# A fused window attention and SwiGLU kernel on one core: group 1 loaded and transposed earlier, sink tables on GpSimd

## The chip, the core and the metric

The kernel runs on one core of a Trainium2 chip. A core has five engines that work side by side, each through its own instruction list in order: TensorE (PE in the profile, its weight loads PEld), VectorE (DVE), ScalarE (ACT), GpSimd (POOL) and SyncE (SP). GpSimd issues most of the loads here, because they turn float32 in memory into bfloat16 on the chip; SyncE issues stores, transposing transfers and a few small loads. Products of TensorE land in PSUM, of which the kernel uses eight banks.

The metric is the device time of one execution, in microseconds (us). The time before is the median of nine executions.

## The reference

Attention of 4 batches, 8 heads, 768 tokens and head size 64, with a window of 128 tokens and 4 sink tokens that every later token sees, and behind it a gated feed-forward block:

```python
scores = scale * np.matmul(q, k.transpose(0, 1, 3, 2))
keep = (pos[None, :] < n_sink) | ((rel >= 0) & (rel < window))
a = softmax(np.where(keep, scores, -1e9))
x = np.matmul(a, v).transpose(0, 2, 1, 3).reshape(B * S, H * D)   # 3072 x 512
g = x @ w_gate                                                    # 512 x 1536
out = (g * sigmoid(g) * (x @ w_val)) @ w_out                      # 1536 x 512
```

Inputs and output are float32; the kernel multiplies in bfloat16.

## The kernel before

**Groups.** The tokens form 12 groups of 256, three for each batch; group g is batch g // 3. Attention goes by groups, in steps whose names the lists below use:

- `step_T(g, ph)`: transposes of keys and queries by TensorE (L257), half of the heads for each `ph`; the key half is copied out of PSUM by ScalarE, the query half by VectorE (L263). Groups 0 to 3 only. Later groups are transposed by transfers on SyncE's queue (`cross_T`, L285; in the lists it is `C(g)`).
- `step_S(g, p2)`: scores of four heads (L323), their exponentials on ScalarE (four of them, L330), and the multiplication with the window mask on VectorE (two of them, L335).
- `step_K(g)`: scores against the four sink tokens of the batch (L346) and their exponential `es` (L350). Not for the first group of a batch, whose window mask holds the sinks. `step_ks(b)` makes the sink keys, and, on VectorE (L300), `vsb`: the sink values laid out so that one product adds them for four heads. It multiplies `vcf`, which eight small loads on SyncE's queue fill (L190), with the pattern `diag_h`.
- `step_PV(g, j, hh)`: probabilities times values for one half of the heads and one tile of 128 tokens; where sinks apply, the product with `es` and `vsb` comes first in the accumulation. The result is divided by the row sum, on VectorE (L375, L382), or on ScalarE where `act` is set (L378).
- `step_X(g, j)`: transposes the 128 x 512 result into `xT` (L406), copied out by VectorE (L412) or, with `act`, by ScalarE (L410).

**Chunks.** The feed-forward block takes the tokens in eight chunks of 256 or 512 (`SIZES`). `gate(tb, f)` makes the gate and the value projection of chunk `tb` (L434), a tanh on ScalarE (L441) and two products on VectorE (`u` L447, `ht` L448). `down(tb, ts)` multiplies with `w_out` (L480), and ScalarE copies out (L484).

**Order.** Everything is emitted in an order written out by hand; each engine keeps to it. A preamble does group 0. Then `weave(us, slots(...))` walks over a list `us` of gates and downs; each number in `slots` is a place in that list, and the attention steps named there are emitted inside that gate (between its two projections) or spread over that down. `alone` is a place with attention only. Copies out of PSUM and mask multiplications are put into a list `later`, which `flush` empties, so that they come behind the current gate's own work. `us` here is g0[0], `alone`, three more gates of chunk 0, the six of chunk 1, the last two of chunk 0, and then downs and chunk 2. `warm(n)` issues matmuls on zeros, whose results nobody reads.

**Loads.** GpSimd issues them in the order of the program: k of group 0, v of group 0, the first piece of the two gate weights (`wg0`, `wv0`), k and q of group 1, the second piece, v of group 1, the other weight pieces. q of group 0 comes over the queues of ScalarE and SyncE. Behind the preamble come group 2, `w_out`, groups 3 and 4; `next_load(g)` loads group g + 4. Bank allocation: all PSUM tiles share one rotation of eight.

Of the kernel before, what the change touches and what calls it, by code (L numbers as in the profile page):

```python
# [15 lines left out]
def kernel(  # L16
# [75 lines left out]
    def load4(g):  # L92

        x = natp.tile([P, H, 4 * D], BF16, tag="kq", name="kq")
        for i, src in ((0, k), (1, q)):
            nc.gpsimd.dma_start(
                x[64 * i:64 * (i + 1)], four_tokens(src, g, slice(0, H)))
        nat[g] = x
# [19 lines left out]
    def load_v(g):  # L118
        va = new_v(g)
        b, c = divmod(g, GC)  # L120
        for j in range(2):
            t0 = c * 256 + j * P
            nc.gpsimd.dma_start(  # L123
                va[:, j, :, 0:D], v[b, :, t0:t0 + P].rearrange("h m d -> m h d"))
# [3 lines left out]
    def load_gate(i):  # L128
        f0, n = sum(FCH[:i]) * P, FCH[i] * P
        for lst, w, nm in ((wgs, moe_w_gate, "wg"), (wvs, moe_w_val, "wv")):  # L130
            t = wpool.tile([P, DMC, n], BF16, tag=f"{nm}{i}", name=nm)
            nc.gpsimd.dma_start(
                t, w[:, f0:f0 + n].rearrange("(c p) f -> p c f", p=P))
            lst.append(t)
# [3 lines left out]
    def load_out(i):  # L138
        n = DFC // 4
        t = wpool.tile([P, n, DM], BF16, tag=f"wo{i}", name="wo")  # L140
        nc.gpsimd.dma_start(
            t, moe_w_out[i * n * P:(i + 1) * n * P].rearrange("(c p) f -> p c f", p=P))
        wos.append(t)
# [25 lines left out]
    for p in range(NP2):  # L169
# [11 lines left out]
    nc.gpsimd.iota(tk, [[0, 1]], base=0, channel_multiplier=1,  # L181
                   allow_small_or_imprecise_dtypes=True)
    load_v(0)
    load_gate(0)

    nc.vector.memset(vcf, 0.0)
    nc.vector.memset(vcf[:, :, D:D + 1], 1.0)
# [5 lines left out]
    for ks in kss:  # L193
# [7 lines left out]
    nc.gpsimd.affine_select(  # L201
        out=dh, in_=dh, compare_op=ALU.is_ge, fill=0.0, base=NS - 1,
        pattern=[[32, NP2], [NS, 2]], channel_multiplier=-1)
    load4(1)
    load_gate(1)
    load_v(1)
    for i in range(2, 5):
        load_gate(i)

    def build_masks():  # L210
# [12 lines left out]
    kTs, qTs, es_t, e_t, xns, xTs = {}, {}, {}, {}, {}, {}  # L223
    later = []

    def flush():
        for f in later:
            f()
        later.clear()

    def warm(n):

        ps = bank([P, 512], FP32, "wm")
        for _ in range(n):
            nc.tensor.matmul(ps, wm[:, 0:P], wm, start=True, stop=True)

    def step_T(g, ph):

        if ph == 0:
            new_kq(g)  # L240
        own = lambda i, p: nat[g][:, 2 * p:2 * p + 2]
        transpose(g, ph, own, (ident, ident))

    def new_kq(g):
        kTs[g] = kqtp.tile([P, NP2, 256], BF16, tag="kT", name="kT")
        qTs[g] = kqtp.tile([P, NP2, 256], BF16, tag="qT", name="qT")

    def transpose(g, ph, rows, ids):


        pts = [bank([P, 2, 64, 4], FP32, "pt") for _ in range(2)]
        for p in range(2):
            for r in range(4):
                for h in range(2):
                    for i in range(2):
                        o = slice(64 * i, 64 * (i + 1))
                        nc.tensor.matmul(  # L257
                            pts[i][64 * h:64 * (h + 1), p, :, r],
                            rows(i, 2 * ph + p)[o, h, r * D:(r + 1) * D],
                            ids[i][o, o], start=True, stop=True)  # L260
        for i, (dst, copy) in enumerate(((kTs, nc.scalar.copy),
                                         (qTs, nc.vector.tensor_copy))):
            copy(out=dst[g][:, 2 * ph:2 * ph + 2],  # L263
                 in_=pts[i].rearrange("q a m r -> q a (m r)"))

    def keys(b, t, r, p):

# [22 lines left out]
    def step_ks(b):  # L290

        dst = kss[b].rearrange("q (a m) -> q a m", m=KS)
        for h in range(2):
            r = slice(h * D, (h + 1) * D)
            nc.vector.tensor_copy(
                out=dst[r, :, h * NS:(h + 1) * NS],
                in_=kTs[b * GC][r, :, 0:NS] if b * GC < NPE
                else cross[b * GC][r, 0, 0, :, 0:NS])
        vsb = const.tile([P, H, D + 1], BF16, tag=f"vsb{b}", name="vsb")
        nc.vector.tensor_tensor(  # L300
            vsb,
            vcf[:, b:b + 1].broadcast_to([P, H, D + 1]),
            diag_h.rearrange("q (h o) -> q h o", o=1).broadcast_to([P, H, D + 1]),
            op=ALU.mult)
        vsbs.append(vsb)

    def step_S(g, p2):

        b, c = divmod(g, GC)
# [42 lines left out]
    def step_PV(g, j, hh, act=False):  # L352
        b, c = divmod(g, GC)
        t = 2 * c + j
        if hh == 0:
            xns[g, j] = xnp.tile([P, DM], BF16, tag="xn", name="xn")
        po = bank([P, 4, D + 1], FP32, "o")
        mms = []
        if c > 0:
            mms.append((po, es_t[g][:, j * P:(j + 1) * P],  # L360
                        vsbs[b][:, 4 * hh:4 * hh + 4]))
        for hq in range(4):
            h = 4 * hh + hq
            if t > 0:
                vp = vas[g][:, 0, h, 0:D + 1] if j else vas[g - 1][:, 1, h, 0:D + 1]
                mms.append((po[:, hq], e_t[g][:, h, 256 * j:256 * j + P], vp))
            mms.append((po[:, hq], e_t[g][:, h, 256 * j + P:256 * (j + 1)],
                        vas[g][:, j, h, 0:D + 1]))
        for i, (o, l, r) in enumerate(mms):
            nc.tensor.matmul(o, l, r, start=(i == 0), stop=(i == len(mms) - 1),  # L370
                             skip_group_check=True)

        def dve():
            rcp = smallp.tile([P, 4, 1], FP32, tag="rcp", name="rcp")
            nc.vector.reciprocal(rcp, po[:, :, D:D + 1])  # L375
            if act:
                for h in range(4):
                    nc.scalar.activation(  # L378
                        xns[g, j][:, (4 * hh + h) * D:(4 * hh + h + 1) * D],
                        po[:, h, 0:D], AF.Copy, scale=rcp[:, h])  # L380
                return
            nc.vector.tensor_tensor(  # L382
                xns[g, j][:, 256 * hh:256 * (hh + 1)].rearrange(
                    "p (h d) -> p h d", h=4),
                po[:, :, 0:D], rcp.broadcast_to([P, 4, D]), op=ALU.mult)
        later.append(dve)
        if hh == 1 and g >= NXPE:
            later.append(lambda: nc.sync.dma_start(
                x_tile(g, j), xns[g, j], transpose=True))
# [106 lines left out]
    def downs(tb):  # L496
        return [(down, tb, t) for t in range(SIZES[tb] // P)]

    def A(fn, *a):
        return lambda: fn(*a)  # L500

    def next_load(g):
        if g + 4 < NG:
            (load4 if g + 4 < NPE else load1)(g + 4)
# [2 lines left out]
    def sinks(b):  # L507
        return [lambda: later.append(A(step_ks, b))]

    def T(g):  # L510
        def last():
            step_T(g, 1)
            next_load(g)
        return [A(step_T, g, 0), last]

    def Ss(g):
        return [A(step_S, g, p2) for p2 in range(2)]

    def PVs(g):

        return [A(step_PV, g, j, hh) for hh in range(2) for j in range(2)]

    def Xs(g):
        return [A(step_X, g, j) for j in range(2)]

    def K(g):
        return A(step_K, g)
# [6 lines left out]
    def pro(*steps):  # L534
        for s in steps:
            s()
            if len(later) > 1:
                later.pop(0)()
# [9 lines left out]
    def C(g):  # L548

        def last():  # L550
            cross_T(g)
            next_load(g)
        return [last]
# [11 lines left out]
    step_S(0, 0)  # L565
    warm(1)
    step_S(0, 1)
    warm(3)
    pro(*[lambda: None] * 3)
    step_PV(0, 0, 0)  # L570
    step_PV(0, 1, 0)
    flush()
    step_PV(0, 1, 1, True)
    step_PV(0, 0, 1)
    flush()
    warm(2)
    pro(A(step_X, 0, 0), A(step_X, 0, 1, True))
    flush()
    warm(2)
    step_ks(0)  # L580
    load4(2)
    load_v(2)
    for i in range(4):
        load_out(i)
    for g in (3, 4):
        (load4 if g < NPE else load1)(g)
        load_v(g)


    g0, g1, g2 = gates(0), gates(1), gates(2)  # L590
    us = [g0[0], (alone, 0, 0), *g0[1:4], *g1, *g0[4:6], downs(0)[0], *g2,
          downs(0)[1], *downs(1), *downs(2)]
    p1 = [A(step_PV, 1, j, hh, j == 1) for hh in range(2) for j in range(2)]
    weave(us, slots(
        (0, T(1)), (1, Ss(1) + [K(1)]), (3, p1 + [flush]),
        (4, [A(step_X, 1, 0), A(step_X, 1, 1, True), flush]),
        (8, T(2)), ((9, 10), Ss(2)), (10, [K(2)]),
        (11, PVs(2)[:2] + [flush]), (12, PVs(2)[2:] + [flush]), (12, C(4)),
        (13, [A(step_X, 2, 0), A(step_X, 2, 1, True), flush]),
        (14, T(3)), ((15, 16), Ss(3)), (16, sinks(1)), ((17, 17, 18, 18), PVs(3)),  # L600
        (18, C(5)), (19, Xs(3)), ((20, 21), Ss(4)), (21, [K(4)]),
        ((22, 22, 23, 23), PVs(4)), (24, Xs(4))))


    def pair(ga, gb, sh=0):
        s = sh
# [46 lines left out]
```

## Time and profile before

| What | Value |
|---|---|
| Median of nine runs | 248.35 us (247.96 to 249.72) |
| Profiled execution | 249.72 us, its span 248.0 us |
| PE busy | 235.1 us, 95% of the span |
| DVE busy | 162.0 us, 65% |
| ACT busy | 112.4 us, 45% |
| POOL busy | 66.6 us, 27% |
| Granted clock of TensorE, mean | 0.991 |
| Loads on GpSimd's queue | 13.90 MB, last one issued near 119 us |

The profile shows one execution. Its span begins with the first instruction and is 1.7 us shorter than the time that the device reports. A row of a timeline gives start, length, engine, line of the kernel, what is written and read, and in brackets how long the engine had stood still and what ended that. Slices cut the span into 40 equal parts of 6.2 us; a digit is the busy share in tenths.

### The profile page before, as it was taken

What the parts mean: (1) busy time and instruction counts of PE and PEld (TensorE: products, weight loads), DVE (VectorE), ACT (ScalarE), POOL (GpSimd) and SP (SyncE); (2) the same over time, 40 slices, a digit from 0 to 9 for tenths busy, and PEclk for the clock granted to TensorE, in tenths of its full rate; (3) what the DMA queues carried; (4) which work ended last, traced back from release to release, by engine and by line L of the source; (5) the groups of instructions that cost most, each with busy time, mean ns of one, the idle gap of its engine ahead of it and who ended that gap; (6) DMA issues with size and microseconds to landing.
All of it is one profiled execution on the core that took longest, in us unless ns stands there. A gap on an engine that the chain in (4) does not pass through costs nothing.

```text
span 248.0 us, 5200 instructions
## 1 busy us (share of the span) xinstructions
PE 235.1 (95%) x2073; PEld 135.8 (55%) x2086; DVE 162.0 (65%) x341; ACT 112.4 (45%) x225; POOL 66.6 (27%) x88
## 2 busy tenths in 40 slices
PE   7689999999699999999999999999999999999994
PEld 3457786778435544544445454445454445488443
DVE  2777888859734288893298991199981289887100
ACT  2658548166063256541564721555611662333111
POOL 8956264893499208005200000000000000000000
PEclk9999999999889999999999999999999999999999
DMA  7999999999999999547990143900244200200132
GB/s 137 151 184 198 203 191 203 159 147 162 152 155 193 184 189 95 36 83 104 221 146 1 41 89 90 210 0 1 45 85 127 87 0 3 42 0 3 42 127 86
DMA packets 97704, 27.11 MB, mean 109 GB/s; under 512 B 83728, under 2 KB 94736, under 8 KB 97680
## 3 DMA queue, kind: packets, MB, share of 16 engines
q0 software_dynamic: 68832, 13.90, 68.4%
q1 hardware_dynamic: 28416, 12.49, 24.0%
q10 hardware_dynamic: 432, 0.39, 0.5%
q8 instruction: 16, 0.26, 0.5%
q14 instruction: 8, 0.07, 0.1%
HBM read 28.34 MB, written 6.29 MB: 140 GB/s over the span
## 4 chain that ended last, share of the span: by engine, by line
PE 77%; DVE 11%; ACT 6%; issue 2%; DMA 2%; POOL 0%; DVEq 0%; POOLq 0%
PE pd L480 24%; PE pv L434 22%; PE pg L434 20%; PE o L370 5%; ACT e L330 4%; DVE ht L448 3%; PE s L323 3%; DVE e L335 2%; DMA kq<-in_k_dram 2%; DVE u L447 2%; DVE xn L382 2%; PE pt L257 2%; PE pd L461 1%; PE px L406 1%; ACT xn L378 1%
## 5 line engine op out<-in xcount | busy, mean ns | idle before, releaser
L434 PE MATMUL pv<-xT,wv 128*128 128x256 bf16 (+1 forms) x384 | 74.8, 328 | 0.9 <-DVE ht L448 0.7
L434 PE MATMUL pg<-xT,wg 128*128 128x256 bf16 (+1 forms) x384 | 74.2, 326 | 0.2 <-ACT xT L410 0.2
L441 ACT ACTIVATE th<-pg 128x512 f32<-128x512 f32 x72 | 43.5, 607 | 61.4 <-PE pg L434 60.8
L447 DVE SCALAR_TENSOR_TENSOR u<-th,pg 128x512 bf16<-128x512 f32 x72 | 49.1, 682 | 30.0 <-ACT th L441 29.6
L480 PE MATMUL pd<-wo,ht 128*128 128x512 bf16 x264 | 63.6, 384 | 0.8 <-issue 0.2
L448 DVE TENSOR_TENSOR ht<-u,pv 128x512 bf16<-128x512 bf16 x72 | 49.5, 687 | 10.4 <-PE pv L434 3.8
L434 PEld LDWEIGHTS <-wg 128*128 128x128 bf16 x384 | 37.5, 98 | 26.0 <-issue 0.6
L330 ACT ACTIVATE e<-s 128x512 bf16<-128x512 f32 (+1 forms) x96 | 45.9, 580 | 7.5 <-PE s L323 7.4
L434 PEld LDWEIGHTS <-wv 128*128 128x128 bf16 x384 | 34.6, 98 | 20.9 <-issue 2.7
L480 PEld LDWEIGHTS <-ht 128*128 128x128 bf16 x276 | 26.2, 99 | 29.1 <-issue 1.4
L484 ACT ACTIVATE ot<-pd 128x512 f32<-128x512 f32 x23 | 13.8, 599 | 49.2 <-PE pd L480 49.1
L335 DVE TENSOR_TENSOR e<-e,mask 128x1024 bf16<-128x1024 bf16 (+1 forms) x48 | 29.3, 641 | 6.6 <-ACT e L330 6.4
L107 POOL DMA_DIRECT2D kq<-in_k_dram x16 | 14.2, 890 | 31.6 <-DMA kqT<-kq 26.9
L123 POOL DMA_DIRECT2D va<-in_v_dram x24 | 21.3, 896 | 4.5 <-DMA kq<-in_q_dram 2.5
L370 PEld LDWEIGHTS <-e 128*128 128x128 bf16 x352 | 16.3, 98 | 7.0 <-DVE e L335 2.0
L382 DVE TENSOR_TENSOR xn<-o,rcp 128x256 bf16<-128x256 f32 x45 | 19.1, 424 | 1.5
L370 PE MATMUL o<-va,e 128*128 128x65 bf16 x352 | 17.9, 193 | 1.3 <-DVE e L335 1.3
L107 POOL DMA_DIRECT2D kq<-in_q_dram x16 | 14.2, 890 | 5.7 <-DMA wo<-in_moe_w_out_dram 2.3
L375 DVE RECIPROCAL rcp<-o 128x4 f32<-128x4 f32 x48 | 8.2, 174 | 8.4 <-PE o L370 8.4
L263 DVE CAST qT<-pt 128x512 bf16<-128x512 f32 x8 | 5.2, 687 | 8.2 <-PE pt L257 8.1
L465 DVE TENSOR_SCALAR ot<-pd 128x256 f32<-128x256 f32 x1 | 0.4, 425 | 14.4 <-PE pd L461 14.4
L370 PE MATMUL o<-vsb,es 128*128 128x260 bf16 x32 | 8.8, 275 | 0.7 <-ACT es L350 0.7
(60 smaller groups left out, 107.9 us busy)
## 6 DMA issues: line engine op xcount, KB each, us to landing
out_dram<-ot SPq DMA_DIRECT2D x23, 256.0 KB
va<-in_v_dram POOLq DMA_DIRECT2D x24, 128.0 KB, 8.7
kq<-in_k_dram POOLq DMA_DIRECT2D x18, 128.0 KB, 7.3
kq<-in_q_dram POOLq DMA_DIRECT2D x16, 128.0 KB, 8.0
wo<-in_moe_w_out_dram POOLq DMA_DIRECT2D x4, 384.0 KB, 12.5
wg<-in_moe_w_gate_dram POOLq DMA_DIRECT2D x4, 256.0 KB, 8.8
wv<-in_moe_w_val_dram POOLq DMA_DIRECT2D x4, 256.0 KB, 9.1
kq<-in_k_dram POOLq DMA_DIRECT2D x3, 256.0 KB, 11.5
```

Of the source, the lines that this page charges most:

```text
L107: nc.gpsimd.dma_start(x[:, j, i].rearrange("p (h d) -> p h d", d=D), src[b, :, t0:t0 + P].rearrange("h m d -> m h d"))
L123: nc.gpsimd.dma_start(va[:, j, :, 0:D], v[b, :, t0:t0 + P].rearrange("h m d -> m h d"))
L330: nc.scalar.activation(e_t[g][:, h0 + h, lo:512], pss[2 * pp + h][:, lo:512], AF.Exp, scale=scale)
L335: nc.vector.tensor_tensor(e, e, m[:, :, lo:512].broadcast_to([P, 2, 512 - lo]), op=ALU.mult)
L370: nc.tensor.matmul(o, l, r, start=(i == 0), stop=(i == len(mms) - 1), skip_group_check=True)
L382: nc.vector.tensor_tensor(xns[g, j][:, 256 * hh:256 * (hh + 1)].rearrange("p (h d) -> p h d", h=4), po[:, :, 0:D], rcp.broadcast_to([P, 4, ...
L434: nc.tensor.matmul(ps[:, i * n:(i + 1) * n], ws[fi][:, c, fo * P:(fo + 1) * P], x[:, 0:n // P, c], start=(c == 0), stop=(c == DMC - 1))
L441: nc.scalar.activation(th, pg, AF.Tanh, scale=0.5)
L447: nc.vector.scalar_tensor_tensor(u, th, 1.0, pg, op0=ALU.add, op1=ALU.mult)
L448: nc.vector.tensor_tensor(hts[tb][:, f:f + two].rearrange("p a n -> p (a n)"), u, pv, op=ALU.mult)
L480: nc.tensor.matmul(po, hts[tb][:, f, ts * P:(ts + 1) * P], wos[f // n][:, f % n], start=(f == 0), stop=(f == DFC - 1))
L484: nc.scalar.activation(ot, po, AF.Copy, scale=0.5)
```

## The change

Loads: k and q of group 1 are issued ahead of the first weights, and v of group 1 ahead of the second. The sink tables `vsb` are built by GpSimd instead of VectorE: the table of batch 0 in the preamble, between v of group 1 and the second weights, the other three behind the loads of `w_out`. Group 1 is transposed in the preamble: its first half behind the context products of group 0, with both copies out of PSUM on ScalarE (`q_act`), its second half behind `step_X` of group 0, with the query copy put into `later` (`q_late`). The first half of the scores of group 1 is emitted in the preamble too. Three calls of `warm` (seven matmuls) become one (two), and two copies out of PSUM that ScalarE had in group 0 go to VectorE.

In the list of gates and downs, three gates of chunk 1 now stand ahead of the fourth of chunk 0, and both downs of chunk 0 ahead of chunk 2. The other attention steps have new places: the context products of group 1 in `alone` and the gate behind it, `step_X` of group 3 in a down instead of in the last gate of chunk 2, the first scores of group 4 in that last gate.

```diff
     load_v(0)
+    load4(1)
     load_gate(0)
+    def build_vsb(b):
+        vsb = const.tile([P, H, D + 1], BF16, tag=f"vsb{b}", name="vsb")
+        nc.gpsimd.tensor_tensor(
+            vsb,
+            vcf[:, b:b + 1].broadcast_to([P, H, D + 1]),
+            diag_h.rearrange("q (h o) -> q h o", o=1).broadcast_to([P, H, D + 1]),
+            op=ALU.mult)
+        vsbs.append(vsb)
...
-    load4(1)
-    load_gate(1)
     load_v(1)
-    for i in range(2, 5):
+    build_vsb(0)
+    for i in range(1, 5):
         load_gate(i)
...
+        evict(0, kTs, nc.scalar.copy)
+        q_copy = A(evict, 1, qTs, nc.scalar.copy if q_act else nc.vector.tensor_copy)
+        if q_late:
+            later.append(q_copy)
+        else:
+            q_copy()
...
     step_S(0, 1)
-    warm(3)
+    warm(2)
     pro(*[lambda: None] * 3)
     step_PV(0, 0, 0)
     step_PV(0, 1, 0)
     flush()
-    step_PV(0, 1, 1, True)
     step_PV(0, 0, 1)
+    step_PV(0, 1, 1)
+    step_T(1, 0, q_act=True)
     flush()
-    warm(2)
-    pro(A(step_X, 0, 0), A(step_X, 0, 1, True))
+    step_X(0, 0)
+    step_X(0, 1)
+    step_T(1, 1, q_late=True)
     flush()
-    warm(2)
     step_ks(0)
+    step_S(1, 0)
     load4(2)
     load_v(2)
     for i in range(4):
         load_out(i)
+    for b in range(1, B):
+        build_vsb(b)
...
-    us = [g0[0], (alone, 0, 0), *g0[1:4], *g1, *g0[4:6], downs(0)[0], *g2,
-          downs(0)[1], *downs(1), *downs(2)]
+    us = [g0[0], (alone, 0, 0), *g0[1:3], *g1[0:3], g0[3], *g1[3:6], *g0[4:6],
+          *downs(0), *g2, *downs(1), *downs(2)]
...
-        (0, T(1)), (1, Ss(1) + [K(1)]), (3, p1 + [flush]),
-        (4, [A(step_X, 1, 0), A(step_X, 1, 1, True), flush]),
-        (8, T(2)), ((9, 10), Ss(2)), (10, [K(2)]),
-        (11, PVs(2)[:2] + [flush]), (12, PVs(2)[2:] + [flush]), (12, C(4)),
-        (13, [A(step_X, 2, 0), A(step_X, 2, 1, True), flush]),
-        (14, T(3)), ((15, 16), Ss(3)), (16, sinks(1)), ((17, 17, 18, 18), PVs(3)),
-        (18, C(5)), (19, Xs(3)), ((20, 21), Ss(4)), (21, [K(4)]),
+        (0, [flush, A(step_S, 1, 1), K(1), A(next_load, 1)]), (1, p1[:2]), (2, p1[2:] + [flush]),
+        (3, [A(step_X, 1, 0), A(step_X, 1, 1, True), flush]),
+        (9, T(2)), ((10, 11), Ss(2)), (11, [K(2)]),
+        (12, PVs(2)[:2] + [flush]), (13, PVs(2)[2:] + [flush]), (13, C(4)),
+        (14, [A(step_X, 2, 0), A(step_X, 2, 1, True), flush]),
+        (15, T(3)), ((16, 17), Ss(3)), (17, sinks(1)), ((18, 18, 19, 19), PVs(3)),
+        (18, C(5)), ((20, 21), Ss(4)), (21, Xs(3) + [K(4)]),
         ((22, 22, 23, 23), PVs(4)), (24, Xs(4))))
```

More of the change, by code (lines that the diff above doesn't have):

```diff
@@ L224, with A @@
     later = []
+    def A(fn, *a):
+        return lambda: fn(*a)
     def flush():
@@ L235, in warm, with step_T @@
             nc.tensor.matmul(ps, wm[:, 0:P], wm, start=True, stop=True)
-    def step_T(g, ph):
+    def step_T(g, ph, q_late=False, q_act=False):
         if ph == 0:
@@ L241, in step_T @@
         own = lambda i, p: nat[g][:, 2 * p:2 * p + 2]
-        transpose(g, ph, own, (ident, ident))
+        transpose(g, ph, own, (ident, ident), q_late, q_act)
     def new_kq(g):
@@ L246, in new_kq, with transpose @@
         qTs[g] = kqtp.tile([P, NP2, 256], BF16, tag="qT", name="qT")
-    def transpose(g, ph, rows, ids):
+    def transpose(g, ph, rows, ids, q_late=False, q_act=False):
         pts = [bank([P, 2, 64, 4], FP32, "pt") for _ in range(2)]
@@ L260, in transpose, with evict @@
                             ids[i][o, o], start=True, stop=True)
-        for i, (dst, copy) in enumerate(((kTs, nc.scalar.copy),
-                                         (qTs, nc.vector.tensor_copy))):
+        def evict(i, dst, copy):
             copy(out=dst[g][:, 2 * ph:2 * ph + 2],
                  in_=pts[i].rearrange("q a m r -> q a (m r)"))
+        evict(0, kTs, nc.scalar.copy)
[4 more added lines that the diff above has]
+            q_copy()
     def keys(b, t, r, p):
@@ L298, in step_ks @@
                 else cross[b * GC][r, 0, 0, :, 0:NS])
[L299 to L305, printed above, removed]
     def step_S(g, p2):
@@ L497, in downs @@
         return [(down, tb, t) for t in range(SIZES[tb] // P)]
-    def A(fn, *a):
-        return lambda: fn(*a)
     def next_load(g):
```

## The prediction

> **What bounds the kernel now.** I read the slices first. TensorE is nearly full from the fourth slice to the end, so a saving counts only where a digit is below 9: the first three slices of 6.2 us and the eleventh (62 to 68 us), where the granted clock falls too.
>
> ```profile
> PE   7689999999699999999999999999999999999994
> DVE  2777888859734288893298991199981289887100
> PEclk9999999999889999999999999999999999999999
> ```
>
> Then the eleventh slice by stretches; the columns are the stretch and its length, busy time of PE, PEld, DVE, ACT, POOL with instructions, granted clock, DMA share and GB/s.
>
> ```profile
> 63.00:65.20 2.20, 0.24 (x4) 0.06 (x3) 2.06 (x7) 0.60 (x1) 0.87 (x1) 1.00 2.03 149
> 65.20:66.20 1.00, 0.85 (x10) 0.65 (x11) 0.97 (x2) 0.00 (x0) 0.86 (x1) 1.00 1.62 150
> 66.20:69.60 3.40, 3.18 (x12) 1.44 (x10) 1.40 (x4) 0.00 (x0) 1.90 (x4) 0.50 2.21 155
> ```
>
> PE stands still for 2.0 us while VectorE is full, and then runs 3.40 us at clock 0.50, which costs another 1.7 us. The chain that ended last says for what it waits: VectorE from 55.75 to 65.67 without a break worth naming, ending in the xn that the transposes of group 3 (step_X, slot 19) read.
>
> ```profile
> 59.97 0.70 DVE vsb L300
> 60.67 0.61 DVE u L447
> ...
> 65.23 0.43 DVE xn L382
> 65.67 0.05 issue
> 65.71 0.28 PE px L406 x2
> ```
>
> At the front, the timeline of ScalarE and of the first context product of group 1 (start, length, engine, line):
>
> ```profile
> 15.01 0.58 ACT L410 COPY xT<-px 128x512 bf16<-128x512 bf16 x1 [0.32 <-PE px L406]
> 17.30 1.07 ACT L263 CAST kT<-pt 128x512 bf16<-128x512 f32 x2
> 19.04 4.03 ACT L330 ACTIVATE e<-s 128x512 bf16<-128x512 f32 x8 [0.67 <-PE s L323]
> 22.87 0.47 ACT L350 ACTIVATE es<-pk 128x256 bf16<-128x256 f32 x1
> ...
> 23.40 0.28 PE L370 MATMUL o<-vsb,es 128*128 128x260 bf16 x1 [0.30 <-ACT es L350]
> ```
>
> The first gate starts at 15.65 when xT is there; group 1 then goes through ScalarE (casts, eight exponentials, es) to 23.35, and meanwhile PE has five projections (of eight matmuls, 0.87 us each) to do, so it waits only 0.30 us. Between 15.65 and 28.92 lie those of four chunks, both of g0[0] to g0[3].
>
> **Loads.** On GpSimd's queue k, q of group 1 go ahead of wg0, wv0, and v of group 1 ahead of wg1, wv1. Every one is 0.7 to 0.9 us of issue and the same 512 KB of reading, and they land in order, so positions swap: wg0 landed at 11.1, wv0 12.7, k 14.3, q 15.7. After it k is there at 11.1, q at 12.7, wg0 14.3, wv0 15.7. q is needed at about 12.95, wg0 at 16.1, wv0 at 18.2: no wait, with 0.25 us to spare at q (and another 0.6 us before the idle time behind T(1) is used up). wg1, wv1 come one v later, 18.6 and 20.0 for 16.9 and 18.3; wanted at 21.9. GpSimd's issue is throttled anyway: its wait at 14.62 is for a load eight places earlier, so some 8 us of transfers are queued, and 1.4 us of table building ahead of wg1, or three tables (4.2 us) ahead of group 3's k at 32.46, when w_out transfers reach to 43, leave no transfer engine dry. Cost nothing; without that backlog it would be those 1.4 and 4.2 us late. SP's queue keeps its order except that the transposes of group 4 are issued one unit later (slot 13); they wait for q landing at 51.4 either way, and land near 56, against a use at about 61 (69.8 before).
>
> **Front, step by step.** VectorE, from the mask multiply ending at 12.55: four context evictions of 0.54 to 0.62 (before three, the fourth was on ScalarE) end at 14.73 for 14.26. X copies 0.42 each: 14.75 to 15.17 and, PE's second transposes ending at 15.05, to 15.60. So xT is ready at 15.60 against 15.59: the extra eviction and ScalarE's lost copy cost nothing. PE: T(1,0), half of 1.02, at 12.95 in time that was idle or warm-up matmuls; T(1,1) 15.05 to 15.57; S(1,0) 0.55 to 16.12; then the first gate, 0.47 later than before. ScalarE: cast of the late keys to 16.15, four exponentials (4.03/8 each) to 18.2, tanh (queued behind them) to 18.8, four more to 20.8, es to 21.15 in place of 23.35. PE: projection to 17.0, S(1,1), pk; the value projection takes the bank of the last early exponential and so starts at 18.25, ends 19.2. Next in order is the product with es and vsb: PE waits **2.0 us, 19.2 to 21.2**. Behind it are queued all later projections. From there: 4 products 1.42, projections of g0[1], g0[2] 3.5, X 0.5, no wait that I find (VectorE's and ScalarE's evictions are done 0.2 to 1 us ahead), so g0[2] ends at 26.62. Before, g0[3] ended at 28.92; less its two projections, 1.74, that is 27.17. **Gain 0.55.**
>
> **Tables on GpSimd.** The trace has no such operation on GpSimd. VectorE's row for it is 0.70 us (699 ns). The Trainium skill, GPSIMD Engine Reference, 3. Performance versus the Vector engine, puts a two-input elementwise operation at about 1.96 times VectorE: an estimate of 1.4 us. Ends 0.7 and 3; I take 1.4. It starts at about 10.5 (issue: k, q to 6.8, wg0, wv0 to 8.35, two selects to 8.8, v 1.8), amid these VectorE multiplies:
>
> ```profile
> 10.46 0.56 DVE L335 TENSOR_TENSOR e<-e,mask 128x768 bf16<-128x768 bf16 x1 [0.21 <-ACT e L330]
> 11.22 0.56 DVE L335 TENSOR_TENSOR e<-e,mask 128x768 bf16<-128x768 bf16 x1 [0.21 <-ACT e L330]
> 11.99 0.56 DVE L335 TENSOR_TENSOR e<-e,mask 128x768 bf16<-128x768 bf16 x1 [0.21 <-ACT e L330]
> ```
>
> By these rows they are paced by ScalarE's 0.39 us exponentials, with 0.21 us between, and nothing of GpSimd's shows an effect: delay 0. By the Trainium skill, SBUF — State Buffer, Who interferes with whom, a VectorE instruction with two SBUF inputs and a GpSimd instruction that reads SBUF exclude each other for a whole instruction: with a start at 11.02 and 1.4 us, the last two multiplies run 12.42 to 13.54 in place of 12.55, delay 1.0 (0.3 at 0.7 us, 2.6 at 3 us). No run here shows which. With 0 the sum is 0.35 below what I give, with 1.0 it is 0.65 above. I take 0.35: the front then gains 0.2.
>
> **Slots 15 to 21.** Group 3's steps keep their places beside chunk 2's gates, vsb leaves VectorE (0.70), X(3) goes from the last gate to the down projection behind it, and S(4,0) comes into the last gate. On the old clock times: u, ht and xn of the chain come 0.70 earlier, the last two xn at about 64.4 and 65.0. PE ends g2[5]'s gate projection at 62.93, does S(4,0), 0.55; its value projection gets its bank (eight in rotation) from the first of those xn: waits 63.5 to 64.45, ends 65.3. Before, at full clock, it would have ended at 66.0 + 0.87 = 66.87, with X done (0.45) and S(4,0) not (0.55). **Gain 1.67**: 66.87 - 65.3 + 0.10. X(3) then runs in down projections, where VectorE is 0.2 to 0.4 busy (slices 12 to 14). What is late next: u of g2[5], to about 65.7, which gives a bank to S(4,1) at 65.75: nothing. Behind 68 PE is full to the end, so gains arrive whole.
>
> **Sum.** The profiled execution took 249.72 (span 248.0 and 1.7 around it). Less 1.67, less the low-clock 1.70, less 0.2: 246.15. That execution is the slowest of the nine. Five lie at 247.96 to 248.35, four at 249.22 to 249.72: a distance like the price of one low-clock stretch, so I suppose that the median 248.35 is without it, and only 1.67 and 0.2 are to be had: **246.5**. I keep that, since the median decides.
>
> **Rivals.**
> *One low-clock stretch at the front.* The new 2.0 us wait for es has the size of the one that halved the clock at 66.2. The Trainium skill, TensorE: Matmul & The Clock Gate, What's actually happening, lets the clock fall after an idle window of about 3.4 us: by that this wait does nothing, 246.5. By the row, 1.09 us busy in 3.2 was enough. Against it: the nine times suggest that such a gap does it in half the executions. In most of them: 246.5 + 1.7 = 248.2.
> *Slower: the clock falls twice.* Place: the front, at about 13.6 (three of the 16 warm-up matmuls issued by then are gone, and a delayed mask leaves PE idle near 12 to 13) and again at 21.3. Price 1.7 each. Against gains of 1.85 it makes the kernel slower by 0.75 from 2.6 us on, one and a half stretches. Two: 249.9. For it: PE was busy 2.09 of 3.40 us from 10.0 on, nearer the limit than it looks; against: clock 1.00 there.
> *GpSimd's table is long:* 3 us delays the chain 2.6 instead of 0.35: 248.7. Only its broadcast operands speak for it.
> *The change only moves the wait:* banks held by VectorE's backlog stop PE in g2[5] as long as X(3) did; front even: 248.3. Against: that backlog is itself shorter by 0.70 and X's two copies.
>
> **How the numbers follow.** Forecast 0.50 (own range 245.4 to 247.4), one low stretch 0.20, two 0.12, long table 0.10, only moved 0.08. Bounds of 0.3% (0.75 us, what a measurement of this kernel tells from no change) are 247.6 and 249.1. Faster: 0.50, 0.04, 0, 0, 0.02: 0.56. Same: 0, 0.11, 0, 0.04, 0.05: 0.20. Slower: 0, 0.05, 0.12, 0.06, 0.01: 0.24. Range 245.4 to 249.0: above lie the two stretches and some of the long table, below little.
>
> **What will show it.** First gate at 16.1 to 16.6; es at 21 to 22 and a wait of PE for it; X(3)'s wait gone and clock 1.00 at 66 to 70; a tensor operation of 0.7 to 1.5 us on GpSimd near 10.5 and whether masks move; PE waiting for a bank at g2[5], about 1 us. Wrong if the granted clock is 0.50 at the front, if T(1,0) waits for q, or if PE still waits 2 us in slot 20.

## The result, and the profile after

The changed kernel takes 246.47 us (median of 16 runs, 245.33 to 247.91), the kernel before 248.26 us (53 runs). The two medians divide to 0.9928; the comparison of all runs on record puts the ratio at 0.9913, with a 95% interval of 0.9895 to 0.9932: 0.7% to 0.9% faster. The forecast was 246.5. The profiled execution took 246.13 us, its span is 244.4 us.

The slices of the changed kernel, in the same three rows as for the kernel before:

```profile
PE   7688999999999999999999999999999999999994
DVE  2687778929983489890498980398970489878000
PEclk9979999999999999999999999999999999999999
```

The 6 in PE's eleventh slice is gone, and the 8s of the clock there too. A new 7 stands in the clock's third slice. The stretches that were shown for the kernel before, at the same times (columns as in the prediction):

```profile
63.00:65.20 2.20, 2.20 (x31) 2.01 (x30) 2.00 (x6) 0.60 (x1) 0.88 (x1) 1.00 1.68 128
65.20:66.20 1.00, 1.00 (x14) 0.69 (x13) 1.00 (x2) 0.22 (x1) 0.10 (x1) 1.00 1.60 156
66.20:69.60 3.40, 2.84 (x36) 1.87 (x32) 3.12 (x9) 3.06 (x7) 1.65 (x2) 1.00 1.81 155
```

PE is full where it stood for 2.0 us, and the clock is 1.00 behind it. What is left of the wait shows in the chain that ended last (start, length, what), in the last gate of chunk 2:

```profile
65.07 0.87 PE pg L444 x8
65.95 0.37 PE s L333 x6
66.32 0.69 DVE ht L458
67.00 0.04 issue
67.05 1.03 PE pv L444 x8
```

From the end of the gate projection, 65.94, to the value projection, 67.05, pass 1.11 us, of which the first scores of group 4 take 0.55: a wait of 0.55 on the chain (PE's rows, whose ends are modelled, show 0.41 of it). X of group 3 follows in a down at 69.60 without one.

The front, from ScalarE's and PE's timeline:

```profile
16.30 0.59 ACT L274 CAST kT<-pt 128x512 bf16<-128x512 f32 x1 [1.28 <-PE pt L269]
16.84 2.06 ACT L340 ACTIVATE e<-s 128x512 bf16<-128x512 f32 x4
19.52 2.06 ACT L340 ACTIVATE e<-s 128x512 bf16<-128x512 f32 x4
21.43 0.43 ACT L360 ACTIVATE es<-pk 128x256 bf16<-128x256 f32 x1
...
21.92 0.28 PE L380 MATMUL o<-vsb,es 128*128 128x260 bf16 x1 [1.17 <-ACT es L360]
```

es comes at 21.87 on the chain (23.35 before), and PE waits 1.17 us for it. Ahead of that lies the low clock; two stretches of 3.40 us (same columns):

```profile
12.10:15.50 3.40, 2.34 (x68) 1.63 (x72) 3.07 (x11) 1.19 (x3) 3.01 (x4) 0.98 1.78 171
15.50:18.90 3.40, 3.40 (x52) 2.18 (x40) 2.48 (x8) 2.60 (x5) 3.40 (x6) 0.51 1.44 170
```

The second runs at 0.51. On GpSimd, the table of batch 0 waits for the small loads of the sink values, and the other three stand where they were expected, ahead of group 3's loads:

```profile
12.49 1.23 POOL L188 TENSOR_TENSOR vsb<-vcf,diag_h 128x520 bf16<-128x520 f32 x1 [1.91 <-DMA vcf<-in_v_dram]
...
32.01 3.09 POOL L188 TENSOR_TENSOR vsb<-vcf,diag_h 128x520 bf16<-128x520 f32 x3
```

Because of this wait it comes at 12.49, not near 10.5 as forecast, after the last of the four mask multiplications had begun (12.24 to 12.80). All four are 0.56 us here: in this execution the table held up none of them.

### The profile page after: what moved, and what is told of

It reads as the page before. It is cut to its first block, busy times and chain, and to the rows that moved or that the text cites. A ratio compares the mean times of both kernels' runs of the same rounds, so it can differ in the third digit from the quotient of the medians.

```text
span 244.4 us, 5189 instructions
## 1 busy us (share of the span) xinstructions
PE 233.3 (95%) x2068; PEld 135.7 (56%) x2081; DVE 160.2 (66%) x338; ACT 111.8 (46%) x221; POOL 70.9 (29%) x92
## 3 DMA queue, kind: packets, MB, share of 16 engines
q1 hardware_dynamic: 28416, 12.49, 24.4%
## 4 chain that ended last, share of the span: by engine, by line
PE 82%; DVE 6%; ACT 5%; DMA 3%; issue 2%; POOL 0%; DVEq 0%; POOLq 0%; ACTq 0%
PE pd L490 24%; PE pv L444 24%; PE pg L444 23%; PE o L380 5%; ACT e L340 3%; PE s L333 3%; DMA kq<-in_k_dram 2%; PE pt L269 2%; DVE ht L458 1%; DVE xn L392 1%; DVE u L457 1%; DVE e L345 1%; ACT th L451 1%; PE px L416 1%; DMA out_dram<-ot 1%
## 5 line engine op out<-in xcount | busy, mean ns | idle before, releaser
L490 PE MATMUL pd<-wo,ht 128*128 128x512 bf16 x264 | 62.7, 379 | 0.5
L458 DVE TENSOR_TENSOR ht<-u,pv 128x512 bf16<-128x512 bf16 x72 | 49.5, 687 | 10.5 <-PE pv L444 3.1
L274 DVE CAST qT<-pt 128x512 bf16<-128x512 f32 x7 | 4.6, 688 | 8.6 <-PE pt L269 8.6
L475 DVE TENSOR_SCALAR ot<-pd 128x256 f32<-128x256 f32 x1 | 0.4, 425 | 14.4 <-DMA out_dram<-ot 14.4
```

What stands on the lines that cost most here:

```text
L458: nc.vector.tensor_tensor(hts[tb][:, f:f + two].rearrange("p a n -> p (a n)"), u, pv, op=ALU.mult)
L490: nc.tensor.matmul(po, hts[tb][:, f, ts * P:(ts + 1) * P], wos[f // n][:, f % n], start=(f == 0), stop=(f == DFC - 1))
```

## The experiments

The theory was that the gain lies in slots 15 to 21 and that the front is about even, a new wait for es and a low clock paying for the earlier transposes. The rival was that the gain comes from the front. Medians are given first; where runs of one kernel bunch by their mean granted clock (1.000 with no low stretch; one stretch of 3.4 us at half clock takes 0.007 off the mean of 245 us), that is said.

**X of group 3 back in the gate.**

```diff
-        (18, C(5)), ((20, 21), Ss(4)), (21, Xs(3) + [K(4)]),
+        (18, C(5)), ((20, 21), Ss(4)), (20, Xs(3)), (21, [K(4)]),
```

> The changed kernel with one edit undone: step_X of group 3 stands again in the last gate of chunk 2 (slot 20) behind the first scores of group 4. Theory (the gain lies in slots 15 to 21): PE waits again for the last xn of group 3, from about 66.3 to 68.1 in place of 66.3 to 67.05 of the changed kernel's trace, so 1.0 us is lost, and another 1.7 where the clock falls behind the wait; time about 247.5 to 248.2. Rival (the gain lies at the front, in the earlier loads and transposes): X(3) costs nothing here, 246.4 to 246.6.

Measured: 247.18 us (10 runs), 0.7 above the changed kernel. PE's rows around it:

```profile
68.79 0.27 PE L416 MATMUL px<-ident,xn 128*128 128x128 bf16 x2 [0.41 <-DVE ht L458]
69.35 0.83 PE L416 MATMUL px<-ident,xn 128*128 128x128 bf16 x6 [0.28 <-DVE xn L392]
70.02 1.04 PE L444 MATMUL pv<-xT,wv 128*128 128x256 bf16 x8
```

From the end of the gate projection (67.70 on the chain) to this value projection pass 2.32 us, less 0.55 for scores and 0.45 for X: a wait of 1.3 where the changed kernel has 0.55. The 0.7 is less than the expected 1.0, and the time lies 0.3 below the range; the clock stayed at 1.00 behind this wait in this trace. At equal clock (0.990 to 0.993, seven runs here and eight of the changed kernel) the difference of the medians is 0.7 to 0.8 too. Moving X is worth 0.7 once the scores of group 4 stand in front of it. The rival, that it costs nothing, falls.

The front of this kernel is that of the changed one, and this trace has two low stretches there: the clock is 0.50 about 15 us, and again 0.50 from 24 to 26 us, behind a wait of 2.11 us for es.

**The back half alone.** The kernel before with its own loads, front and tables, and a list in which both downs of chunk 0 stand ahead of chunk 2:

```diff
-    us = [g0[0], (alone, 0, 0), *g0[1:4], *g1, *g0[4:6], downs(0)[0], *g2,
-          downs(0)[1], *downs(1), *downs(2)]
+    us = [g0[0], (alone, 0, 0), *g0[1:4], *g1, *g0[4:6], *downs(0), *g2,
+          *downs(1), *downs(2)]
...
-        (14, T(3)), ((15, 16), Ss(3)), (16, sinks(1)), ((17, 17, 18, 18), PVs(3)),
-        (18, C(5)), (19, Xs(3)), ((20, 21), Ss(4)), (21, [K(4)]),
+        (15, T(3)), ((16, 17), Ss(3)), (17, sinks(1)), ((18, 18, 19, 19), PVs(3)),
+        (18, C(5)), ((20, 21), Ss(4)), (21, Xs(3) + [K(4)]),
```

> The kernel before with the back half of the change alone: both downs of chunk 0 ahead of chunk 2, X(3) in a down, the first scores of group 4 in the last gate of chunk 2; loads, front and tables as before, so VectorE still builds the table of batch 1. Theory: the old front is even with the new one, so nearly the whole gain is here; the bank wait in slot 20 is 0.73 (measured in the changed kernel) plus the table's 0.70: 246.5 to 247.3, and clock 1.00 at 66 to 72. Rival front: 248.0 to 248.4.

Measured: 246.35 us (7 runs), ratio to before 0.9933 (0.9908 to 0.9958). Between medians that is all of the changed kernel's gain, with the old front; the rival falls. (Six of the seven runs have a mean clock of 0.997 or more, against four of the changed kernel's 17: what the new front is worth at equal clock is worked out below.) In the last gate of chunk 2 PE waits twice, for VectorE's u and ht, as expected with a table in VectorE's backlog:

```profile
66.03 0.21 PE L323 MATMUL s<-kqT,kT 64*128 64x128 bf16 x1 [0.34 <-DVE u L447]
66.03 0.37 PE L323 MATMUL s<-kqT 64*128 64x256 bf16 x4
66.82 1.03 PE L434 MATMUL pv<-xT,wv 128*128 128x256 bf16 x8 [0.41 <-DVE ht L448]
```

**Warm-up matmuls at the front.** The changed kernel with

```diff
-    warm(2)
+    warm(3)
     pro(*[lambda: None] * 3)
     step_PV(0, 0, 0)
     step_PV(0, 1, 0)
+    warm(2)
...
     step_T(1, 0, q_act=True)
+    warm(2)
```

> The changed kernel with five warm-up matmuls on zeros put back into the front's gaps (one more behind the first scores, two behind the first context products of group 0, two behind the first transposes of group 1). Theory: the clock of 0.50 from 15.5 to 18.9 in the changed kernel's trace comes from the missing warm-up; with them the front runs at 1.00, es comes about 0.5 us earlier and runs bunch lower: 245.5 to 246.0. Rival (the clock falls whatever stands in the gaps, or the matmuls delay the transposes): 246.4 to 247.0.

Measured: 245.76 us (9 runs, 245.39 to 247.65). Five of the nine have a mean clock of 0.997 or 1.000 and took 245.39 to 245.76; the other four have 0.990 to 0.993 and took 246.76 to 247.65. So the matmuls do not always keep the clock up. Of the changed kernel's 17 runs (the profiled one included) four had 0.997 or more; five of nine against that is too few to be sure of, but the two kernels below that have the matmuls and the sink scores first had it in eleven of eleven. The profiled run had 1.00 throughout, and its front is the one that the prediction worked out. PE's timeline:

```profile
16.29 1.05 PE L444 MATMUL pg<-xT,wg 128*128 128x256 bf16 x8
...
18.04 1.05 PE L444 MATMUL pv<-xT,wv 128*128 128x256 bf16 x8
21.19 0.28 PE L380 MATMUL o<-vsb,es 128*128 128x260 bf16 x1 [2.10 <-ACT es L360]
```

PE stands 2.10 us for es, and the clock stays at 1.00 behind it here. At the low clock of the changed kernel the same wait is 1.17: the slower matmuls run in part in time in which PE would wait.

**Sink scores first.**

```diff
-        (0, [flush, A(step_S, 1, 1), K(1), A(next_load, 1)]), (1, p1[:2]), (2, p1[2:] + [flush]),
+        (0, [flush, K(1), A(step_S, 1, 1), A(next_load, 1)]), (1, p1[:2]), (2, p1[2:] + [flush]),
```

> The changed kernel with step_K of group 1 ahead of the second half of its scores, so that ScalarE makes es before the last four exponentials. Theory: PE's wait for es (1.17 us at low clock, 2.0 worked out at full clock) is the price of the new front; es comes 2.0 us earlier, PE waits instead about 1 us for the masks of the late heads, so 0.5 to 1.0 us is gained: 245.4 to 246.0. Rival (what PE waits for is only exchanged): 246.3 to 246.7.

Measured: 245.33 us (4 runs, 244.79 to 245.72), just below the expected range. es is there at 20.20 although the front ran at low clock here, and from 14 to 30 us PE's only waits are 0.43 for a mask multiplication and 0.38 for an xn of group 0. At equal clock the four runs lie about 0.7 below the changed kernel's; the rest of the 1.1 between medians is that two of four, and not four of 17, ran without a low stretch. The wait for es was a price, not an exchange.

This trace shows what the changed kernel's did not. The table on GpSimd and the last mask multiplication of group 0 on VectorE:

```profile
11.38 1.36 POOL L188 TENSOR_TENSOR vsb<-vcf,diag_h 128x520 bf16<-128x520 f32 x1 [0.84 <-issue]
12.03 1.12 DVE L345 TENSOR_TENSOR e<-e,mask 128x768 bf16<-128x768 bf16 x1 [0.21 <-ACT e L340]
```

The table began 0.65 us before the multiplication, which took 1.12 instead of 0.56 and ended 0.42 behind the table. In the trace with X back in the gate it is the same: table 11.67 to 12.73, multiplication from 11.93, 1.22 us.

**Both edits**, warm-up and sink scores first:

> Both edits of the two runs before on the changed kernel: five warm-up matmuls back at the front, and step_K of group 1 ahead of the second half of its scores. Theory (the low clock and the wait for es are separate prices): what each gave alone against 246.47 adds up in part, 0.7 for the clock and 1.1 for es, of which the run with step_K first still had a low clock in its trace: 244.4 to 245.1, clock 1.00 from 14 to 19. Rival (one price, seen twice): no lower than 245.3.

Measured: 245.15 us (6 runs, 244.53 to 245.35), mean clock 0.998 to 1.000 in all six. It is lower than either alone, by 0.2 and 0.6, and lies between the range of the theory and the rival's bound of 245.3. The two runs with sink scores first that had no low stretch, 244.79 and 245.02, are as fast: what the matmuls add is that the low stretch stays away, in all of six runs. That the two prices are separate fits this, but 0.2 between six and four runs does not show it.

**GpSimd beside the masks.** The kernel with the warm-up matmuls, and behind `load_v(1)`, with results that nobody reads:

```diff
+    for i in range(2):
+        spare = const.tile([P, H, D + 1], BF16, tag=f"spare{i}", name="spare")
+        nc.gpsimd.tensor_tensor(
+            spare,
+            tq[:, 0:D + 1].rearrange("q (o d) -> q o d", o=1).broadcast_to([P, H, D + 1]),
+            diag_h.rearrange("q (h o) -> q h o", o=1).broadcast_to([P, H, D + 1]),
+            op=ALU.mult)
     build_vsb(0)
```

> The changed kernel with the five warm-up matmuls and with two more multiplications on GpSimd, of the table's shape, right behind the loads of group 1's values, on operands that are there by then; nothing reads their result. They run from about 10.6, amid VectorE's four mask multiplications of 0.56 us. If both engines exclude each other: a mask multiplication of 1.0 us or more, the last one ends up to 1 us later than 12.8, the first gate starts later by as much, time 245.8 to 246.8 against 245.76 with the warm-up alone. If they do not: masks stay at 0.56, time 245.6 to 245.9.

Measured: 249.72 us (10 runs, 248.18 to 250.69), 4 us above its neighbour without them. VectorE's and GpSimd's rows (the rows of one line are merged):

```profile
9.86 5.05 DVE L352 TENSOR_TENSOR e<-e,mask 128x768 bf16<-128x768 bf16 x4 [0.49 <-ACT e L347]
10.54 2.47 POOL L217 TENSOR_TENSOR spare<-tq,diag_h 128x520 bf16<-128x520 f32 x2
12.97 1.05 POOL L188 TENSOR_TENSOR vsb<-vcf,diag_h 128x520 bf16<-128x520 f32 x1
```

The four multiplications end at 14.91 instead of 12.7; one took 2.43 us, one 0.55. The engines exclude each other, as the Trainium skill, SBUF — State Buffer, Who interferes with whom, has it, and the delay is well beyond the 1 us that I had allowed. In the trace the masks end 2.2 us later; besides, the mean clock was 0.977 to 0.993 in all ten runs, probably because of the gaps that this left on PE. The five runs with 0.990 to 0.993 took 248.18 to 249.31, the other five 250.12 to 250.69. How much of the 4 us each of the two is worth was not separated.

**Tables on VectorE again**, in `step_ks`, everything else as changed:

```diff
-        nc.gpsimd.tensor_tensor(
+        nc.vector.tensor_tensor(
...
-    build_vsb(0)
...
+        build_vsb(b)
...
-    for b in range(1, B):
-        build_vsb(b)
```

> The changed kernel with the four sink tables built by VectorE again, in step_ks. Theory: the 0.70 us of table 1 lies in VectorE's backlog ahead of slot 20, so PE's wait there grows from 0.73 by 0.4 to 0.7 (1.13 in the run with the old front, which has the table on VectorE); at the front the table costs nothing or delays the first masks of group 1 by less than 0.5: 246.7 to 247.4. Rival (the tables' engine does not matter): 246.3 to 246.6.

Measured: 246.86 us (10 runs). Four runs with mean clock 1.000 took 246.03 to 246.26, the changed kernel's two with 1.000 took 245.33 and 245.48: 0.7 at equal clock. PE's waits from 52 to 85 us (in total, times, longest):

```profile
PE pv L444 <- DVE ht L458: 0.4, 1, 0.4
PE s L333 <- DVE u L457: 0.3, 1, 0.3
```

The first is there in the changed kernel too, the second is not: it is the table in the backlog, as with the back half alone. That is 0.3 of the 0.7; where the rest arises is not shown.

**Old order of loads**, everything else as changed:

```diff
     load_v(0)
-    load4(1)
     load_gate(0)
...
+    load4(1)
+    load_gate(1)
     load_v(1)
     build_vsb(0)
-    for i in range(1, 5):
+    for i in range(2, 5):
```

> The changed kernel with the old order of loads (first weights ahead of group 1's keys and queries, second weights ahead of its values), everything else as changed. Theory: q of group 1 lands at about 15.7; the transposes of group 1 stand ahead of step_X of group 0 in PE's order, so PE waits from 13.3 to 15.7, first gate at about 18.4 in place of 16.3 to 17.2, es about 2 us later: 247.8 to 248.8. Rival (the loads' order is no part of it, because transfers are ahead of their use): 246.3 to 246.7.

Measured: 248.41 us (10 runs, ratio to before 0.9993, 0.9966 to 1.0019): as slow as before.

```profile
15.63 1.06 PE L270 MATMUL pt<-ident,kq 64*64 64x64 bf16 x31 [1.29 <-DMA kq<-in_q_dram]
16.63 1.04 PE L417 MATMUL px<-ident,xn 128*128 128x128 bf16 x8
```

The transposes wait for q until 15.6, X of group 0 behind them until 16.6, the first gate starts at 19.56, and all ten runs have a mean clock of 0.983 to 0.986, which is what two low stretches make. Without the new order the early transposes lose 1.9 us, the lower clock included. (The last two masks were held up here too, 1.19 and 1.41 us; q lands later than they end, so this does not matter. Why the first of them waited is open: it began 0.9 us before the table's row.)

**The table later.** Both edits, and `build_vsb(0)` behind the second and third pair of weight loads:

```diff
-    build_vsb(0)
     for i in range(1, 5):
         load_gate(i)
+        if i == 2:
+            build_vsb(0)
```

> The kernel with both edits (warm-up matmuls, step_K first) and the table of batch 0 two pairs of weight loads later on GpSimd's queue, at about 13.6 instead of 10.7 to 12.5, behind the last mask multiplication of group 0 (12.7). If the exclusion of the two engines is what is left of the tables' price: all four mask multiplications at 0.56 us, last one ending 0.1 to 0.6 earlier, time 244.5 to 245.0 against 245.15. If not: 245.0 to 245.4.

Measured: 244.44 us (5 runs, 244.29 to 244.57), ratio to before 0.9832 (0.9806 to 0.9858), a little below the range. The last mask multiplication and the table, and the same with both edits alone (two multiplications in a row):

```profile
11.81 0.56 DVE L346 TENSOR_TENSOR e<-e,mask 128x768 bf16<-128x768 bf16 x1 [0.21 <-ACT e L341]
...
13.55 1.08 POOL L188 TENSOR_TENSOR vsb<-vcf,diag_h 128x520 bf16<-128x520 f32 x1
```

```profile
10.75 1.06 POOL L188 TENSOR_TENSOR vsb<-vcf,diag_h 128x520 bf16<-128x520 f32 x1 [0.21 <-issue]
11.06 1.63 DVE L345 TENSOR_TENSOR e<-e,mask 128x768 bf16<-128x768 bf16 x2 [0.21 <-ACT e L340]
```

With the table later all four multiplications are 0.56, and the last ends at 12.37. In the run with both edits the first of the two took 1.16 us, and the last ended at 12.69. These two traces explain 0.3 of the 0.7 between the medians, and their times, 244.38 and 244.69, differ by as much; in other executions of the run with both edits the collision may have cost more, as the 1.12 and 1.22 above did, which no trace of that kernel shows. This version is 1.7% faster than the kernel before and 0.8% faster than the changed one.

## Why the prediction was right

The time and the sign were right, and most of the working too, but two terms were wrong in opposite directions, by about 1 us and by 0.8. That they cancel to 0.03 us is luck, and one of the forecast's own signs of being wrong, a clock of 0.50 at the front, came about (0.51).

**Median against profile: right.** The supposition was that the slowest four of nine runs had a low-clock stretch. Of 29 runs of the kernel before that were made beside four of the experiments, 16 with a mean clock of 0.997 to 1.000 took 247.77 to 248.66, 13 with 0.991 to 0.993 took 249.04 to 250.41.

**Slots 15 to 21: right in size, one step wrong in detail.** 1.67 was forecast. The back half alone, with the table still on VectorE, gave 1.9 between medians. In the traces: from the end of g0[2] to the first gate of chunk 3 the kernel before needs 85.01 - 27.17 = 57.84 (27.17 as worked out in the prediction), the changed one 81.74 - 27.45 = 54.29; less 1.70 for the low clock, 1.85. The remaining wait was put at 0.95, because the value projection's bank should come from an xn; it came from ht of the gate before, which VectorE finishes ahead of that xn, and the wait was 0.55.

**Front: right where the clock is 1.00.** The run with warm-up matmuls has the first gate at 16.29 (forecast 16.12), es at 21.14 (21.15), PE's wait from 19.1 to 21.19 (19.2 to 21.2) and the end of g0[2] at 26.72 (26.62). The changed kernel's own trace ends g0[2] at 27.45, 0.28 behind the old front, and not 0.2 ahead of it.

**Loads cost nothing: right.** In the changed kernel's trace no transpose of group 1 and no projection waits for a transfer. What does is the table of batch 0, for the sink values, 1.91 us on GpSimd, which I had thought landed by then; it held up nothing. That the early transposes need this order, the old order shows: 1.9 us.

**The first wrong term: the low clock.** The likeliest case had none at the front; the rival with one had a fifth. In 13 of 17 runs the mean clock was 0.993 or less, so one or more was the rule. It did not cost 1.7: the eight runs with 0.990 to 0.993 took 245.87 to 246.87, about 1 us above the two at 1.000. The traces offer a reason, the wait for es of 1.17 in place of 2.10, but with sink scores first, without that wait, the low clock cost no more (about 0.8, four runs): the reason is not shown. The other five, with 0.984 to 0.986, took 246.45 to 247.91; theirs is the clock of two low stretches. Nor did it come where I looked for it, behind the wait for es: in the changed kernel's trace it begins near 15.4, before that wait. I had named that neighbourhood (13.6) only in the rival with two stretches. With X back in the gate, on the same front, the trace has both, and the second lies behind the wait for es as that rival had it; in the warm-up run's trace a wait as long, 2.10, brought no fall.

**The second wrong term: the gain at full clock, too small by 0.8.** 1.87 was forecast (1.67 and 0.2). By medians at full clock: before 248.1, back half alone 246.3, tables on VectorE with the new front 246.1, changed kernel 245.4 (two runs): 2.7. The steps are 1.8 for the back half, 0.2 for the new front, 0.7 for the tables. By the traces, two terms of the sum were too dear. One is the wait for the bank, 0.55 in place of 0.95. The other is the 0.35 charged for GpSimd's table at the front, which the changed kernel's trace did not pay. The multiplication takes 1.06 us alone (estimate 1.4), and what it costs depends on when it falls: the last mask ended 0, 0, 0.3, 0.6 and 0.7 us late in the five traces that have the table at this place and the new order of loads. So 0.35 is near the mean of these traces; what the two runs at full clock paid, no trace shows. Moving the table away, behind both edits, gains 0.7.

With about 1 us of low clock on the median, 245.4 becomes 246.47.

Of the rivals, "only moved" is refuted (PE's wait of 1.96 by its rows became 0.41), the 3 us table too (1.06). The clock of one low stretch is that of eight of the changed kernel's 17 runs, at a lower price than the rival had. The clock of two is that of five of them, and of all ten with the old order of loads; with the spare GpSimd work one of ten has it, and four lie lower still.

## What to carry to other kernels

A step put earlier into PE's order was worth nothing here until its data came earlier too (248.41 with the old loads), and it then hit the next engine in the chain: ScalarE's eight exponentials, behind which a small one was queued that PE needed first. Ask of each queue what the waiting instruction stands behind, and put the small early need first: exchanging two entries of a list gave 0.7 at equal clock, the whole new front 0.2. Work moved to GpSimd was not free beside VectorE's multiplications of two on-chip operands; moved past them, it held up nothing.

## What was not expected of the hardware

- TensorE's clock fell to 0.51 behind a stretch in which PE's rows are 2.34 of 3.40 us busy (12.1 to 15.5, mostly transposes of 64 columns, the longest pause 0.53), while the kernel before kept 1.00 behind 2.09 busy in the same stretch, with four warm-up matmuls of 512 columns in it. A busy share by rows does not say when it falls. Nor does the number of columns streamed: counted from the rows of this stretch it is some 4,900 where the clock fell, 3,700 in the kernel before and 6,500 in the warm-up run, where it did not. What counts stays open. The stretch in the kernel before and in the warm-up run:

```profile
12.10:15.50 3.40, 2.09 (x22) 1.10 (x21) 2.90 (x11) 1.41 (x5) 2.18 (x3) 1.00 1.44 193
12.10:15.50 3.40, 2.56 (x79) 1.82 (x81) 3.17 (x11) 1.09 (x3) 2.31 (x3) 1.00 1.81 166
```

- A wait of PE of some 2 us was followed by half clock in the kernel before (1.96, at 65 us) and with X back in the gate (2.11, at 22 us), and not in the warm-up run (2.10, at 21 us). Which it will be, no number looked at here tells.
- Exclusion between GpSimd and VectorE stretched a mask multiplication of 0.56 us to as much as 2.43 us. Of the three GpSimd operations in a row, the multiplication waited through the rest of the second and the whole third: it began at 12.0 and ended near 14.4, 0.4 behind the third.
- Eight small loads on SyncE's queue, issued by 7.4 us, were there only at about 12.4 us in the changed kernel's trace, beside the large loads; in the run with both edits the table that waits for them began at 10.75.
